# A fused attention and expert kernel: its front end as a list of timed steps, ordered inside the kernel

## The chip, the cores and the metric

The kernel runs on one core of a Trainium2 chip. The metric is device time in microseconds (us) for one execution; lower is better. A run's time is that of the whole program; the profiled execution also gives the span from its first to its last instruction.

## What is computed

Three layers follow each other. An attention with 32 memory slots turns q, k, v and phi (4 batches, 8 heads, 576 rows, 64 columns) into x, 2304 tokens of 512 numbers. A layer of eight experts then sends each token to its two best experts. A last layer multiplies, applies g = h cos h and multiplies again.

```python
a = softmax(phi, axis=rows)                     # 4 x 8 heads, 576 x 32
k_m, v_m = a^T k, a^T v                         # 32 x 64 for each head
x = softmax(q k_m^T / 8) v_m                    # 2304 tokens x 512
noisy = x @ w_gate + log1p(exp(x @ w_noise)) * noise
top2 = two largest of noisy                     # with weights from their softmax
out[token] = sum over its two experts of weight * (relu(x @ w1[e]) @ w2[e])
h = out @ w_in;  result = (h * cos(h)) @ w_out
```

## The kernel before, in words

**Keys.** For each of the four batches `k_gen` takes the maximum of phi on VectorE (DVE), the exponential on ScalarE (ACT), transposes the weights on TensorE (`et`), multiplies them with the batch's five row tiles of k and v in one matmul of 128 columns (`kp`), scales (`kd`, `vm`), transposes the keys (`pk`) and lays them block by block into `bdk`. The values go into `bdv`, four heads of a group side by side and masked, and 16 routing columns are appended. `sb` and `sT` hold a power of two by which x is scaled.

**Tiles.** For each of 18 tiles of 128 tokens `t_gen` does the scores (`sc`, TensorE), their maximum and subtraction (DVE: `smx`, `sd`), the exponential (ACT), the sum and its reciprocal (DVE: `ssm`), the product (`d`, GpSimd, called POOL here), a transpose (`pt`), its copy (`e2T`, ACT), the product with the values (`x`, two matmuls of 272 columns for a whole tile), the scaled copy (`xs`), the routing columns (`lgb` or `rt`), a 16-bit copy (`hl`, ACT), the rest of it (`hl` again, POOL), and a store to `xd` in memory. Tiles 4 and 13 hold rows of two batches.

**Routing.** `route(0)` handles tiles 0 to 7, `route(1)` tiles 8 to 17: a chain of some 40 small DVE steps that ends in tables made on TensorE (`rank`, then `tab` out of `ohp` and `oha`), and from them token lists `idxA` and `idxB`. POOL gathers the listed rows (`xg`) by an indirect transfer; a transposing transfer on the SP queue turns them into `x`.

**Experts.** Expert e works on part 0 (two blocks of 128 tokens, from tiles 0 to 7 alone) and part 1 (three blocks): `l1` (matmul `h`, eight groups of 12 matmuls for part 0) and `l2` (matmul `y`). Its weights are split into a 16-bit part `w` made on ACT after a sum of squares (`junk`, `sums`, `wsc`) and a rest made on DVE. Expert 0's part 0 runs before route(1) is done (`l2_first`), and from its part 1 on the TensorE has work without end.

**Order.** Every step has a time written out by hand (`a_of`, `t_steps`, `k_start`, `k_steps`); steps are recorded in the order of these times. Some instructions are also held behind a named earlier one (`gated`). Loads stand in a fixed list on SP's queue.

Of the kernel before, what the change touches and what calls it, by code (L numbers as in the profile page):

```python
# [60 lines left out]
def fused_kernel(ctx, tc, phiT, qT, kv, wgn, noise, w1, w2, wi, wo, out):  # L61
# [14 lines left out]
    line = []  # L76
    LEAD = dict(l1=60.0, l2=60.0, l1_out=60.0, l2_out=60.0, gather_x=50.0, turn_x=50.0)
# [36 lines left out]
    V.tensor_scalar(after, jp, 0.0, -1.0, op0=OP.is_le, op1=OP.mult)  # L114
    ones = sm([P, P], F16, "ones")
# [129 lines left out]
    def w_lo(i, c):  # L245
        scaled_lo(wt[i][:, 1, PIECE[c]], piece(i, c), wt[i][:, 0, PIECE[c]], i)
# [95 lines left out]
    def route(g):  # L342
# [4 lines left out]
        u, w1p, l, c, y = (rg(g, k, n, E) for k in "uwlcy")  # L347
        lgp = rg(g, "lgp", n, 2 * E)
        V.tensor_tensor(lgp, lgb[g][:, :, 0], lgb[g][:, :, 1], op=OP.add)
        gate, z = lgp[:, :, 0:E], lgp[:, :, E:]  # L350
        last["u"] = V.scalar_tensor_tensor(u, z, -1.0, z, op0=OP.mult, op1=OP.max)
        A.activation(u, u, AF.Exp, scale=-1.0)
        yield
        last["w1p"] = V.tensor_scalar(w1p, u, 1.0, None, op0=OP.add)
        last["ln"] = A.activation(l, w1p, AF.Ln)
        yield
        V.scalar_tensor_tensor(c, w1p, 1.0, u, op0=OP.subtract, op1=OP.subtract)
        V.reciprocal(w1p, w1p)
        V.tensor_tensor(c, c, w1p, op=OP.mult)
        V.scalar_tensor_tensor(c, z, 0.0, c, op0=OP.max, op1=OP.subtract)  # L360
        yield
        V.tensor_tensor(l, l, c, op=OP.add)
        V.tensor_tensor(l, l, noise_sb[:, ts, :], op=OP.mult)
        V.tensor_tensor(y, l, gate, op=OP.add)
        yield
        mk = [rg(g, f"m{k}", n) for k in range(2)]
        kx = rg(g, "k", n)
        for k in range(2):
            V.tensor_reduce(mk[k], y, axis=AX.X, op=OP.max)
            yield  # L370
            V.tensor_tensor(c, y, bc_t(mk[k], n), op=OP.is_equal)
            yield
            V.tensor_tensor(c, c, bc_e(ekey, n), op=OP.mult)
            yield
            V.tensor_reduce(kx, c, axis=AX.X, op=OP.max)
            yield
            V.tensor_tensor(oh[k][:, ts, :], c, bc_t(kx, n), op=OP.is_equal)
            yield
            if k == 0:
                V.scalar_tensor_tensor(y, oh[0][:, ts, :], -3.0e38, y, op0=OP.mult, op1=OP.add)  # L380
                yield
        last[f"m16{g}"] = V.tensor_tensor(m16[:, ts, :], oh[0][:, ts, :], oh[1][:, ts, :], op=OP.add)
        d = rg(g, "d", n)
        V.tensor_tensor(d, mk[1], mk[0], op=OP.subtract)
        A.activation(d, d, AF.Exp)
        yield
        r = mbank("rank")
        w = n * E
        mv = m16[:, ts, :].rearrange("p t e -> p e t")
        T.matmul(r[:, 0:w], lhsT=after, rhs=mv, start=True, stop=False, skip_group_check=True)  # L390
        T.matmul(r[:, 0:w], lhsT=ones, rhs=e32[:, :, :n], start=False, stop=True, skip_group_check=True)
# [881 lines left out]
```

## Time and profile before

| what | value |
|---|---|
| median of three runs | 926.5 us (925.14 to 928.25) |
| the profiled execution, its own time | 926.95 us |
| its span | 925.1 us |
| TensorE (PE) busy | 879.5 us, 95% of the span |
| DVE, ACT, POOL busy | 582.4, 467.7, 215.4 us |

The profiled execution's own time is 1.85 us more than its span. An engine's busy time counts its instructions, not its waits. The granted clock is TensorE's: 1.00 stands for 2.4 GHz and 0.50 for 1.2 GHz.

### The profile page before, as it was taken

The page shows a single profiled execution, that of the slowest core. Times are in us where ns is not written, and L with a number is a line of the kernel's source. Part 1 is how long each engine was busy: PE and PEld are TensorE (multiplying, and loading weights), DVE is VectorE, ACT ScalarE, POOL GpSimd, SP SyncE. Part 2 cuts the span into 40 slices and gives each one's busy share as a digit, 9 for nine tenths or more (in the row PEclk, how much of TensorE's full clock was granted, in tenths as well). Part 3 has the DMA queues.
Part 4 walks back from the last instruction along what each step waited for, and adds up shares of the span by engine and source line. Part 5 has one row for each costly group of instructions (what it writes and reads, how often), then busy time and mean ns, then how long its engine had stood idle before and what let it go on. Part 6 is the DMA issues. An engine that isn't in the chain of part 4 may idle for free. (4 is left out here: it accounts for less than half of the span.)

```text
span 925.1 us, 14179 instructions
## 1 busy us (share of the span) xinstructions
PE 879.5 (95%) x5368; PEld 511.0 (55%) x5368; DVE 582.4 (63%) x1266; ACT 467.7 (51%) x830; POOL 215.4 (23%) x234
## 2 busy tenths in 40 slices
PE   5997499999999999999999998999999999999997
PEld 4875355746566574756555565664444444444564
DVE  3668753766657575766571377787875765554564
ACT  3588426666666676777761334444333432422242
POOL 1355222110201101020000034434322521322221
PEclk9897599999999999999999999999999999999999
DMA  9982469787778979696762553322301610200010
GB/s 353 395 300 86 114 167 263 240 291 236 237 257 252 289 242 282 231 307 247 205 216 93 171 160 58 95 52 72 80 1 12 149 23 12 68 12 1 1 46 23
DMA packets 108246, 146.55 MB, mean 158 GB/s; under 512 B 65808, under 2 KB 66448, under 8 KB 106128
## 3 DMA queue, kind: packets, MB, share of 16 engines
q1 hardware_dynamic: 89536, 103.56, 36.5%
q0 software_dynamic: 6080, 19.93, 7.5%
q10 hardware_dynamic: 12560, 22.13, 6.7%
q8 instruction: 43, 0.70, 0.3%
q14 instruction: 27, 0.22, 0.1%
HBM read 95.26 MB, written 35.13 MB: 141 GB/s over the span
## 5 line engine op out<-in xcount | busy, mean ns | idle before, releaser
L219 PE MATMUL h<-x,w 128*128 128x384 f16 (+1 forms) x1536 | 215.3, 302 | 9.8 <-DMA x<-xg 9.2
L219 PE MATMUL y<-w,hT 128*128 128x512 f16 x960 | 210.7, 379 | 2.2 <-issue 2.2
L219 PE MATMUL g<-x2T,win 128*128 128x256 f16 (+1 forms) x1152 | 203.8, 327 | 5.5 <-DVE ty L1048 4.9
L219 PE MATMUL o<-wout,gT 128*128 128x512 f16 x864 | 202.5, 380 | 0.3 <-POOL gT L1050 0.2
L219 PEld LDWEIGHTS <-w 128*128 128x128 f16 x1536 | 151.5, 99 | 68.9 <-DMA x<-xg 8.8
L219 PEld LDWEIGHTS <-win 128*128 128x128 f16 x1152 | 113.2, 98 | 89.8 <-issue 6.8
L219 PEld LDWEIGHTS <-hT 128*128 128x128 f16 x960 | 93.9, 99 | 111.4 <-issue 2.7
L1050 POOL TENSOR_TENSOR gT<-ty,gT 128x256 f16<-128x256 f32 (+1 forms) x96 | 92.9, 968 | 253.8 <-ACT gT L1049 249.9
L1047 ACT ACTIVATE tt<-tt,hp 128x256 f32<-128x256 f32 (+1 forms) x96 | 58.9, 614 | 163.8 <-DVE tt L1046 147.7
L219 PEld LDWEIGHTS <-gT 128*128 128x128 f16 x864 | 84.4, 98 | 93.8 <-POOL gT L1050 1.9
L219 DVE SCALAR_TENSOR_TENSOR w<-raw,wsc,w 128x1024 f16<-128x1024 f32 x64 | 81.1, 1288 | 32.8 <-ACT w L219 31.2
L219 DVE SCALAR_TENSOR_TENSOR hT<-h,hT 128x384 f16<-128x384 f32 (+1 forms) x128 | 61.4, 487 | 61.9 <-ACT hT L219 61.7
L1044 DVE SCALAR_TENSOR_TENSOR ty<-g,wis,bct 128x256 f32<-128x256 f32 (+1 forms) x96 | 58.9, 613 | 65.1 <-PE g L219 65.1
L219 ACT ACTIVATE hT<-h 128x384 f16<-128x384 f32 (+1 forms) x128 | 55.2, 435 | 74.3 <-PE h L219 70.2
L1048 DVE SCALAR_TENSOR_TENSOR ty<-g,fac,tt 128x256 f32<-128x256 f32 (+1 forms) x96 | 59.1, 616 | 53.0 <-ACT tt L1047 52.5
L1049 ACT ACTIVATE gT<-ty 128x256 f16<-128x256 f32 (+1 forms) x96 | 50.2, 523 | 66.0 <-DVE ty L1048 65.9
L829 POOL DMA_INDIRECT xg<-xd,idxB x24 | 25.1, 1045 | 218.3 <-DMA x<-xg 206.9
L219 ACT ACTIVATE w<-raw,wsc 128x1024 f16<-128x1024 f32 x64 | 71.6, 1140 | 4.1 <-DVE wsc L219 1.9
L219 ACT ACTIVATE junk<-raw 128x1024 bf16<-128x1024 f32 x64 | 67.3, 1052 | 3.8 <-ACT o L219 2.5
L1046 DVE SCALAR_TENSOR_TENSOR tt<-tt,ty 128x256 f32<-128x256 f32 (+1 forms) x96 | 67.5, 703 | 2.6
L219 ACT ACTIVATE o<-y,ysc 128x512 f32<-128x512 f32 x40 | 27.5, 687 | 73.3 <-PE y L219 73.3
L968 POOL DMA_INDIRECT y<-yd,sidx x36 | 36.2, 1004 | 88.4 <-DMA yd<-o 80.7
(234 smaller groups left out, 712.8 us busy)
## 6 DMA issues: line engine op xcount, KB each, us to landing
raw<-in_w SPq DMA_DIRECT2D x32, 1024.0 KB, 11.4
yd<-o ACTq DMA_DIRECT2D x40, 256.0 KB, 6.8
kvt<-in_kv SPq DMA_DIRECT2D x9, 1024.0 KB
cvt<-in_wi SPq DMA_DIRECT2D x8, 1024.0 KB
wst<-cvt SPq DMA_DIRECT2D x16, 512.0 KB
cvt<-in_wo SPq DMA_DIRECT2D x8, 1024.0 KB, 8.6
yd<-zero ACTq DMA_DIRECT2D x13, 512.0 KB, 7.1
xd<-hl SPq DMA_DIRECT2D x18, 256.0 KB, 2.0
```

Of the source, the lines that this page charges most:

```text
L219: last[key] = fn(*a, **kw)
L829: G.indirect_dma_start(out=g, out_offset=None, in_=xd[0:NA * P] if part == 0 else xd, in_offset=bass.IndirectOffsetOnAxis(ap=idx[:, col:co ...
L968: G.indirect_dma_start(out=y, out_offset=None, in_=yd[0:rows], in_offset=bass.IndirectOffsetOnAxis(ap=sidx[:, t, k:k + 1], axis=0))
L1044: V.scalar_tensor_tensor(y, ph[:, :n], wis[:, 2 * E + c:2 * E + c + 1], bct[j], op0=OP.mult, op1=OP.mult)
L1046: V.scalar_tensor_tensor(t, t, MAGIC, y, op0=OP.subtract, op1=OP.subtract)
L1047: A.activation(t, t, AF.Sin, bias=hp, scale=-2.0 * math.pi)
L1048: V.scalar_tensor_tensor(y, ph[:, :n], fac[:, c:c + 1], t, op0=OP.mult, op1=OP.mult)
L1049: A.activation(g[:, 0, :n], y, AF.Copy)
L1050: G.tensor_tensor(g[:, 1, :n], y, g[:, 0, :n], op=OP.subtract)
```

## The change

The generators and the hand-written times of the front end go. Each step (one key step, one tile step, one route step, one load) becomes an entry of a list: engine, duration, function, the entries that it waits for. `settle` lays the entries out engine by engine, forwards and backwards in turn, and keeps the layout in which expert 0's part 1 starts earliest. Every instruction of a step is then chained to the one before it on its engine, so that this order stands in the program.

```diff
+    def op(eng, cost, fn, *deps, lat=None):
+        ...
+        plan.append((eng, cost, fn, [d for d in flat if d is not None], LAT[eng] if lat is None else lat))
+        return len(plan) - 1
+    def settle(goal):
...
+        best = now = place([-x for x in tail], before)
+        for _ in range(ROUNDS):
+            end = place([-(t + c) for t, c in zip(now, cost)], after)
+            last_end = max(t + c for t, c in zip(end, cost))
+            now = place([last_end - t - c for t, c in zip(end, cost)], before)
+            if now[goal] < best[goal]:
+                best = now
+        for i in sorted(range(n), key=lambda i: (best[i], i)):
+            if plan[i][2]:
+                at(best[i], plan[i][2])
```

Beside the order these things change.

```diff
 first batch: keys of three row blocks are loaded before their values; its kp becomes kp and vp, 64 columns each
+    def load_kv(j, half=None):
...
+        cs = slice(0, 2 * DM) if half is None else slice(half * DM, half * DM + DM)
+        load(kvt[j][:, :, cs], kv[2 * j * P:2 * (j + 1) * P, cs].rearrange("(t p) d -> p t d", p=P))
 values: halves of the contraction rows
-        bv = ap.tile([P, 2, 272], F32, tag="bdv", name="bdv")
+            x = bdv[b] = ap.tile([P, 2, 144], F32, tag="bdv", name="bdv")
-                    last[f"t{t}P"] = T.matmul(x[pn, g, 0:272], lhsT=eT[:, g, pn], rhs=bdv[b][:, g, :], start=True,
-                                              stop=True)
+                    for j in range(2):
+                        pj = slice(64 * j, 64 * j + 64)
+                        chain("P", T.matmul, c["x"][pn, j, 144 * g:144 * g + 144], lhsT=c["eT"][pj, g, pn],
+                              rhs=bdv[b][pj, g, :], start=True, stop=True)
 from other engines to POOL: the 16-bit copy of tiles 6 to 13, sT, the product with tokb
+            if t in HI_POOL:
+                chain("G", G.tensor_copy, c["hv"][:, 0], c["xs"])
+            else:
+                chain("A", A.activation, c["hv"][:, 0], c["xs"], AF.Copy)
-        V.tensor_copy(sT[:, :, full[0]:full[-1] + 1], sb[:, :, None].to_broadcast([P, 2, n]))
+            chain("G", G.tensor_copy, sT[:, :, full[0]:full[-1] + 1], s[:, :, None].to_broadcast([P, 2, n]))
-            V.tensor_tensor(oha, oha, tokb[:, tt, None, None].to_broadcast([P, m, 2, nc_]), op=OP.mult)
+                chain("G", G.tensor_tensor, x, x, tokb[:, t:t + m, None, None].to_broadcast([P, m, 2, nc_]), op=OP.mult)
 TensorE is given 21 matmuls of 512 columns before there is data
+    def keep_busy(n):
+        w = mbank("busy")
+        for k in range(n):
+            chain("P", T.matmul, w, lhsT=ones, rhs=ones[:, None, :].to_broadcast([P, 4, P]), start=True, stop=True,
+                  skip_group_check=True)
+    o_busy = op("P", 6.2, lambda: keep_busy(21))
 expert 0, part 1: the gathered rows are turned on TensorE, no longer by a transposing transfer
+    def turn_on_pe(e, part, c):
+        z = turned[c] = bank_y().bitcast(F16).rearrange("p (k t) -> p k t", k=8)
+        for k in range(8):
+            chain("P", T.transpose, z[:, k, :], xg[e, c][:, k * P:(k + 1) * P], ident16)
+    def turn_out(e, part, c, half):
...
+        if half:
+            chain("V", V.tensor_copy, xT[e, part][:, ks, cs], turned[c][:, ks, :])
+        else:
+            chain("A", A.activation, xT[e, part][:, ks, cs], turned[c][:, ks, :], AF.Copy)
 what follows is placed from the layout's own start of expert 0, part 1
-    X = [a_end + 0.5]
+    X = [x_first]
```

What the layout makes of three places is seen in the instruction rows; the number at the end of a row says how often it stands.

**TensorE, the first batch.** Before, all products of weights with keys and values come first, then the first keys are turned and the first scores follow:

```order
L577 MATMUL et<-ident,ew 128x128 x10
L589 MATMUL kp<-kvt,e 32x128 x40
L601 MATMUL pk<-ident,kd 128x128 x2
L616 MATMUL pv<-ident,vm 64x128 x2
L659 MATMUL sc<-bdk,qt 128x64 x4
```

Now, behind the 21 matmuls into `busy`:

```order
L291 MATMUL et<-ident,ew 128x128 x8
L291 MATMUL vp<-kvt,e 32x64 x8
L291 MATMUL kp<-kvt,e 32x64 x16
...
L291 MATMUL kp<-kvt,e 32x64 x8
L291 MATMUL vp<-kvt,e 32x64 x8
L291 MATMUL pk<-ident,kd 128x128 x2
L291 MATMUL sc<-bdk,qt 128x64 x4
```

Products with the keys (`kp`) and with the values (`vp`) alternate by row tile, a value product is the first, and the turn of the keys (`pk`) stands behind the last value product.

**POOL, around the first gathers.** Before, both gathers of expert 0's part 0 stand behind the work of all 18 tiles:

```order
L705 TENSOR_TENSOR hl<-xs,hl 128x512
L412 CAST af<-af_125 128x16
L705 TENSOR_TENSOR hl<-xs,hl 128x512 x4
L829 DMA xg<-xd,idxA 128x1024 x2
L412 CAST af<-af_125 128x20
```

Now (`sd_148` is tile 15's, `sd_145` tile 16's, `sd_146` tile 17's):

```order
L291 TENSOR_TENSOR d<-sd_148,ssm 128x256
L291 DMA xg<-xd,idxA 128x1024
L291 TENSOR_TENSOR d<-sd_145,ssm 128x256
L291 TENSOR_TENSOR d<-sd_146,ssm 128x256
L291 DMA xg<-xd,idxA 128x1024
L291 TENSOR_TENSOR hl<-xs,hl 128x512 x4
L291 CAST af<-af_127 128x20
```

The second gather stands right behind tile 17's product, ahead of the last four tiles' `hl`.

**TensorE, the last table of route(1).** Before, the products `tab` are spread among the groups of `h`, and the last two stand ahead of all of `y`:

```order
L219 MATMUL h<-x_1393,w 128x256
L433 LDWEIGHTS ohp
L433 MATMUL tab<-oha,ohp 128x24
L433 LDWEIGHTS ohp
L433 MATMUL tab<-oha,ohp 128x24
L219 LDWEIGHTS hT
L219 MATMUL y<-w,hT 128x512
```

Now 18 of the 20 stand behind all of `h`, and the last two behind 32 of the 48 matmuls of `y`:

```order
L291 MATMUL y<-w,hT 128x512
L291 LDWEIGHTS ohp
L291 MATMUL tab<-oha,ohp 128x24
L291 LDWEIGHTS ohp
L291 MATMUL tab<-oha,ohp 128x24
L291 LDWEIGHTS hT
L291 MATMUL y<-w,hT 128x512
```

`idxB` needs the last `tab`, so it has moved behind 32 matmuls of `y`. The `rank` matmuls of route(1), which stood behind two groups of `h`, now stand behind six.

## Rows read from the trace of the kernel before

**Rows 1.** Windows: us, busy PE, PEld, DVE, ACT, POOL, clock, DMA share, GB/s.

```profile
132.50:925.10 792.60, 778.15 (x4446) 435.86 (x4445) 498.91 (x970) 392.60 (x644) 167.91 (x167) 1.00 0.48 146
...
18.80:30.00 11.20, 11.07 (x129) 8.98 (x128) 4.86 (x19) 3.99 (x11) 1.24 (x2) 0.55 1.04 401
30.00:81.10 51.10, 46.62 (x497) 37.44 (x498) 36.53 (x116) 43.05 (x119) 27.46 (x34) 1.00 0.75 279
81.10:95.50 14.40, 9.39 (x38) 5.82 (x36) 10.45 (x48) 11.68 (x25) 6.38 (x7) 0.51 0.24 91
18.80:81.10 62.30, 57.69 (x625) 46.42 (x624) 41.39 (x134) 47.04 (x130) 28.70 (x36) 0.92 0.80 301
```

**Rows 2.** Timeline of PE, first batch: start, us, instruction, idle before and releaser.

```profile
13.28 2.79 PE L589 MATMUL kp<-kvt,e 128*32 128x128 f32 x48 [0.73 <-DMA kvt<-in_kv]
...
18.79 1.00 PE L659 MATMUL sc<-bdk,qt 128*128 128x64 f32 x8
```

**Rows 3.** Timeline of PE at the full clock, two places where matmuls follow directly.

```profile
41.82 0.64 PE L589 MATMUL kp<-kvt,e 128*32 128x128 f32 x14
42.39 1.10 PE L659 MATMUL sc<-bdk,qt 128*128 128x64 f32 x8
...
51.10 1.14 PE L689 MATMUL x<-bdv,e2T 128*128 128x272 f32 x4
52.08 0.38 PE L577 MATMUL et<-ident,ew 128*128 128x128 f32 x2
```

**Rows 4.** Timelines of DVE and POOL: route steps beside POOL's work, one of them twice.

```profile
69.93 1.11 DVE L354 TENSOR_SCALAR rw<-ru 128x64 f32<-128x64 f32 x1 [0.24 <-ACT ru L352]
...
81.59 0.61 POOL L675 TENSOR_TENSOR d<-sd,ssm 128x256 f32<-128x256 f32 x1 [1.42 <-DVE rc L373]
82.25 1.15 POOL L705 TENSOR_TENSOR hl<-xs,hl 128x512 f16<-128x512 f32 x1
82.32 1.16 DVE L382 TENSOR_TENSOR m<-oh,oh 128x64 f16<-128x64 f32 x1
...
106.32 0.24 DVE L382 TENSOR_TENSOR m<-oh,oh 128x80 f16<-128x80 f32 x1
```

**Rows 5.** Windows of DVE's lines 638, 642 (`sT`) and 427 (`tokb`).

```profile
18.80:81.10 62.30, 1.86 (x4) 0.92 0.80 301
...
18.80:81.10 62.30, 1.57 (x4) 0.92 0.80 301
...
81.10:95.50 14.40, 1.10 (x3) 0.51 0.24 91
```

**Rows 6.** Timelines of DVE, POOL, PE: tile 17's sum to expert 0.

```profile
80.68 0.42 DVE L672 TENSOR_REDUCE ssm<-sd 128x8 f32<-128x264 f32 x1
...
98.54 1.89 POOL L829 DMA_INDIRECT xg<-xd,idxA  x1 [0.30 <-issue]
...
106.43 5.30 PE L219 MATMUL h<-x,w 128*128 128x256 f16 x24 [8.71 <-DMA x<-xg]
```

**Rows 7.** Timelines of PE, DVE, POOL after that, and one landing time.

```profile
111.73 0.31 PE L392 MATMUL rank<-m,ones 128*128 128x80 f16 x1
111.86 4.15 PE L219 MATMUL h<-x,w 128*128 128x256 f16 x36
...
119.71 0.30 PE L433 MATMUL tab<-oha,ohp 128*128 128x24 f16 x6
...
121.52 10.52 PE L219 MATMUL y<-w,hT 128*128 128x512 f16 x48
132.54 2.76 PE L219 MATMUL h<-x,w 128*128 128x384 f16 x16 [0.49 <-DMA x<-xg]
...
121.71 0.18 DVE L441 TENSOR_TENSOR idxB<-tab,tabB 128x24 int32<-128x24 f32 x1 [0.83 <-PE tab L433]
...
124.82 0.94 POOL L829 DMA_INDIRECT xg<-xd,idxB  x1 [0.30 <-issue]
...
xg<-xd,idxB POOLq DMA_INDIRECT x3, 3.6
```

More of the change, by code (lines that the diff above doesn't have):

```diff
@@ L356, in route @@
[L356 to L367, printed above, removed]
@@ L392, in route, with tiles @@
-        last["rank"] = T.matmul(r[:, w:2 * w], lhsT=ones, rhs=mv, start=True, stop=True, skip_group_check=True)
-        yield
-        upto = rg(g, "cum", w)
-        V.tensor_tensor_scan(upto, same[g], r[:, w:2 * w], 0.0, op0=OP.mult, op1=OP.add)
+        w = n * E
+        early = n - 2
+        q = {}
+        def tiles():
+            for k in "uwlcy":
+                q[k] = rg(g, k, n, E)
+            q["lgp"] = rg(g, "lgp", n, 2 * E)
+            q["gate"], q["z"] = q["lgp"][:, :, 0:E], q["lgp"][:, :, E:]
+            q["mk"] = [rg(g, f"m{k}", n) for k in range(2)]
+            q["kx"], q["d"], q["cum"] = rg(g, "k", n), rg(g, "d", n), rg(g, "cum", w)
+            q["vk"], q["den"] = rg(g, "vk", n, 2), rg(g, "den", n)
@@ new lines, in lgp, with make @@
+        def lgp(a, b):
+            def make():
+                if not q:
+                    tiles()
+                return [red(q["lgp"][:, a:b], lgb[g][:, a:b].rearrange("p t s n -> p t n s"), OP.add)]
+            return make
+        o = v(0.9, lgp(0, early), o_rt[t0 + early - 1], *([o_free["rt"]] if g else []))
+        o = v(0.27, lgp(early, n), o, o_rt[t1 - 1])
+        o = v(0.27, lambda: [stt(q["u"], q["z"], -1.0, q["z"], op0=OP.mult, op1=OP.max)], o)
+        o = a_(0.25, lambda: chain("A", A.activation, q["u"], q["u"], AF.Exp, scale=-1.0), o)
@@ new lines, in places, with make, table, run @@
+        def places(t):
+            def make():
+                x = q["ohp", t] = small.tile([P, 2, P], F16, tag="ohp", name="ohp", bufs=4)
+                return [ts_(x[:, k], iota_r, pf[:, t, k:k + 1], None, op0=OP.is_equal) for k in range(2)]
+            return make
+        def table(t, q_):
+            def run():
+                if t == t0:
+                    q["tb"] = mbank("tab")
+                for k in range(2):
+                    chain("P", T.matmul, q["tb"][:, :nc_], lhsT=q["ohp", t][:, k], rhs=q["oha", t - q_][:, q_, k],
+                          start=(t == t0 and k == 0), stop=(t == t1 - 1 and k == 1))
+            return run
@@ new lines, in gather @@
+    def gather(e, part, c):
+        idx = idxA if part == 0 else idxB
+        if c == parts[part][0]:
+            n = parts[part][1] - parts[part][0]
+            xT[e, part] = xp.tile([P, 8, n * P], F16, tag=f"x{part}", name=f"x{part}")
+        xg[e, c] = xp.tile([P, 2 * DM], F16, tag="xg", name="xg", bufs=3)
+        col = e * (parts[part][1] - parts[part][0]) + c - parts[part][0]
+        chain("G", G.indirect_dma_start, out=xg[e, c], out_offset=None, in_=xd[0:NA * P] if part == 0 else xd,
+              in_offset=bass.IndirectOffsetOnAxis(ap=idx[:, col:col + 1], axis=0))
@@ new lines, in fused_kernel @@
+    get_phi(1)
+    keys(0)
+    get_kv(3)
+    get_kv(4)
+    get_q(4, 8)
+    get_phi(2)
+    keys(1)
+    o_free["kv5"], o_free["kv6"] = o_free["used0"], o_free["used1"]
+    for t in range(5):
+        tile_ops(t)
+    get_kv(5)
+    get_kv(6)
+    get_q(8, 12)
+    get_phi(3)
+    keys(2)
+    o_free["rt"] = o_free["used5"]
+    for t in range(5, 9):
+        tile_ops(t)
+    get_kv(7)
+    o_free["kv8"] = o_free["used2"]
+    get_kv(8)
+    get_q(12, 16)
+    get_q(16, 18)
+    get_w(0, 0)
@@ L831, in gather_x @@
             if turn:
[L832 to L834 removed]
+                SP.dma_start_transpose(out=xT[e, part][:, :, (c - c0) * P:(c - c0 + 1) * P], in_=g)
     def turn_x(e, part, c):
```

811 lines of the change are left out of this document (496 added, 315 removed).

## The prediction

> **What bounds the kernel now.** I read the windows first, then the timelines. From 132.50, where expert 0's part 1 starts, TensorE is busy for 778.15 of 792.60 us at the full clock [rows 1]. This stretch keeps its code, so it keeps its 792.6 us, and the question is how much earlier it can start. Ahead of it TensorE is the busiest engine from the first score (18.79 [rows 2]) to the sum of the last tile, tile 17 (80.68 [rows 6]): 57.69 of 62.30 us [rows 1]. But 11.07 of these lie between 18.80 and 30.00, where the granted clock is 0.55, nearly always the lower of its two levels (1.2 GHz), and from 81.10 to 95.50 it is 0.51 [rows 1]. From that sum to expert 0's first matmul at 106.43 TensorE mostly waits; a transfer releases it [rows 6]. A last stretch, 106.43 to 132.54, holds `h`, the last tables and `y`, and ends with three gathers [rows 6, 7]. The change works on all three stretches.
>
> I make the sum against the profiled execution: span 925.1, time 926.95, which lies 0.05% above the median of the three runs. Two times closer than 0.3% (2.8 us) I call the same.
>
> **First score: 16.0 (18.79 before).** Before, the third load of keys and values lands at 13.28, with the products waiting for it [rows 2]; 0.59 + 3 x 1.05 MB have then come. The turn of the keys (`pk`) stands behind the last value product, so loading keys first does not let it start before the last value half. Ahead of that half come the same bytes and one more part of q, 0.52 MB; at 401 GB/s [rows 1] that is 1.3 us, so 14.6. Eight half products, the scale, the turn and its copy: 1.4 us, estimated. Bounds: 14 (the products catch up at once) and 18.8 (no gain).
>
> **First score to tile 17's sum: 56 us (61.9 before).** I take each engine's work in this stretch.
>
> TensorE: 57.69. If its first 11.07 run at the full clock they take half, minus 5.5. The product `x` now has 4 x 144 columns in two halves of the rows, where it had 2 x 272. It took 0.98 (51.10 to 52.08 [rows 3]). No row shows halves of the rows. Halves that follow each other would need as much as before; halves that overlap fully, 0.49. The nearest row is `kp`, which works on quarters of the columns: seven matmuls of 128 columns in 0.57 [rows 3], 0.08 each, while one of 272 columns takes 0.49 (the trace counts two instructions for a matmul of this type). That is a third of the time for its columns, so overlap between parts is real here; I take 0.6, minus 0.38 for some 15 tiles, 5.7. Tables of route(0) that now fall into the stretch: plus 1. Sum 47.5, bounds 42 and 59 (lower clock, no overlap).
>
> DVE: 41.39, and as the whole of route(0) now ends ahead of that sum, the 10.45 of the window behind it too [rows 1]. Moved to POOL: `sT` 1.86 + 1.57, `tokb` 1.10 [rows 5]. That leaves 47.3.
>
> POOL: 28.70 [rows 1]. Added: eight 16-bit copies, which no row shows at this size. Bounds 0.61 (half the elements, two inputs) and 1.16 (the same elements, two inputs [rows 4]); one input and all elements lie between, 0.9, together 7.2. Plus `sT`, `tokb` and one more `hl`, 5.7; minus half of three batches' `bdv`, 1.8. Sum 40: of 56 us 70%, where it was 46%.
>
> That share costs DVE something. A route step that starts while POOL works can last as long as POOL's instruction: the step `m` takes 1.16 beside an `hl` of 1.15 that ends with it, and 0.24 where POOL is idle [rows 4]. From 69.93 to 82.32 there are five such steps [rows 4], which lose about 4 us in all. At 70 instead of 46 that is 6, plus 2: DVE 49.4.
>
> The Trainium skill (SBUF — State Buffer, "Who interferes with whom") gives this as a lock: DVE with two inputs from SBUF, or in a two-port mode, and GpSimd hold a port pair for a whole instruction, and the later one stands still. The `m` row agrees; that only five steps show it does not settle how often. Applied to every route step it speaks against moving work to POOL; its sum is a rival below.
>
> ACT: 47.04, minus eight copies of about 0.6, plus some of the work behind: 45. So DVE becomes the longest. An engine in a chain of four is not full: TensorE before was at 93% [rows 1]. With 88% for DVE, 49.4 / 0.88 = 56. Bounds 51 (93%, no added locks) and 65. Tile 17's sum comes at 16 + 56 = **72**.
>
> **That sum to expert 0's first matmul: 9 us (25.8 before).** The second gather stands on POOL behind tile 17's product: the sum, its reciprocal and 0.61 for the product [rows 4] make 1.2. From that gather's start to the first matmul it took 7.9 (98.54 to 106.43 [rows 6]). So 9.1, and the first `h` at **81**. Beside it lies the splitting of the expert's weights, which now also begins after tile 17's sum: about 0.5 for the scale, 2 for ACT's tile work, four splits, one rest, some 8.4 in all by my estimate. If the gather is quicker, this is late next.
>
> **First `h` to part 1: 34 us (26.1 before).** Here the order costs. `rank` of route(1) stands behind six groups of `h` where it stood behind two. TensorE has waited some 4 us when `h` starts, so I expect the lower clock for the first two groups, as before: 5.30 for 24 matmuls, then 4.15 for 36 [rows 6, 7], that is 5.3 + 5.5 = 10.8. `rank` 0.5. From `rank` (111.73) to the last `tab` but two (120.0) it took 8.3 [rows 7]; `tokb` leaves DVE, so 7.7. Then 32 of 48 matmuls `y`, 7.0 of 10.52 [rows 7], stand ahead of the last `tab`; before, none did. Table and `idxB` 0.4. From `idxB` to the third gather 3.1 (121.71 to 124.82), landing 3.6 [rows 7]: 6.5 counted from its end. Turning on TensorE replaces the transposing transfers: eight transposes and a copy, for which I take 1.3. No row has 16-bit transposes of 128 columns; bounds 0.6 and 2.5. Before, from the landing (128.4) to 132.54 it was 4.1, so this edit gives back 2.8. Sum 10.8 + 0.5 + 7.7 + 7.0 + 0.4 + 6.5 + 1.3 = 34.2.
>
> The 7 us of `y` are not lost to TensorE as work, since `y` had to be done; what is lost is the cover: before, `y` ran while the gathers were under way, now only its last 16 matmuls do. Behind `idxB` on DVE nothing waits; the four rests of expert 0's second weights stand ahead of it (5.2) but end before the 32 matmuls do.
>
> **Sum.** Part 1 starts at 81.1 + 34.2 = 115.3 instead of 132.54: minus 17.2. 926.95 - 17.2 = **910**.
>
> **Rivals.**
>
> *Everything fits.* The 21 early matmuls bring the full clock, no locks are added, DVE runs at 93%: sum of tile 17 at 16 + 51 = 67, first `h` at 76, and at the full clock (six groups in 8.3) 31.7 to part 1. 107.8, minus 24.7: **902**. For it: TensorE, which was the busiest, loses a fifth of its work. Against: all four engines would then be busy above 75% of the stretch.
>
> *The locks, by the page's rule.* If every one of route(0)'s 41 DVE steps that meets POOL (70%) waits for half an instruction of 0.9, that is 13 us where I count 6; the sum comes at 79, `h` at 88, and with `y` too at the lower clock (2.5 more) part 1 starts at 125: **919**. A first batch at the lower clock, as now until 30, would add 5.5 on TensorE, which stays below DVE then.
>
> *Slower.* One mechanism: DVE stands still for whole POOL instructions. `m` lost 0.92. If all 41 steps do, that is 38 us, and part 1 starts at 147: 941. It decides from a loss of 0.64 a step on, where tile 17's sum comes at 92 and part 1 at 135.3. Against it: the five steps counted above lost 4 us together, and they stand among some 25 route steps of the same stretch, so the mean loss before is below 0.2 a step.
>
> *The order does not hold.* A chained order is as good as its durations; a step that is late holds all behind it on its engine. If that takes 17 us in sum, nothing changes: **927**.
>
> **How the numbers follow.** Forecast (905 to 917) 0.49; everything fits (899 to 905) 0.20; locks (917 to 922) 0.16; no change 0.05; slower 0.07; the rest, 0.03, lies below 899. The likeliest is 910. From 900 to 922 about 0.8 lie: the first three without their ends. Faster by more than 0.3% 0.88, same 0.05, slower 0.07.
>
> **What the profile will show.** First score near 16, with the clock at 1.00 between 18 and 30 (TensorE) if the early matmuls work. `x` of a tile in about 0.6. Tile 17's sum near 72, DVE the busiest engine ahead of it, and more route steps of 0.8 and longer beside POOL. The second gather right behind the last `d`. First `h` near 81, part 1 near 115, with TensorE idle between the last `h` and the first `y`. From there 792.6 to the end. The prediction is wrong if the tile stretch is not bound by DVE, or if the rest does not keep its length because expert 1's weights, loaded at another time, come late.

## The result, and the profile after

The changed kernel took **936.25 us** (median of 4 runs, 935.59 to 939.22), the kernel before, run beside it, 926.81 (925.14 to 928.25): a ratio of 1.011, 95% interval 1.008 to 1.014. It is 1.1% slower, where 910 was forecast. The profiled execution is the longest of the four, 939.22 with a span of 937.4.

The forecast was a chain of five stages, so I read them first. The windows of the changed kernel (the stretch and its length, busy time of each engine, granted clock, busy share of the DMA engines, GB/s):

```profile
143.70:937.40 793.70, 781.36 (x4446) 436.69 (x4445) 498.30 (x971) 392.14 (x643) 164.82 (x166) 0.99 0.47 141
21.80:30.00 8.20, 8.20 (x93) 7.33 (x94) 3.20 (x10) 3.62 (x10) 1.23 (x2) 0.60 1.04 397
30.00:60.00 30.00, 26.21 (x358) 21.25 (x356) 21.16 (x61) 24.12 (x69) 15.22 (x24) 1.00 1.03 393
60.00:93.30 33.30, 25.53 (x269) 20.50 (x267) 28.44 (x93) 17.64 (x48) 21.29 (x33) 0.74 0.19 73
```

The engines are in the order TensorE, its weight loads, VectorE (DVE), ScalarE (ACT), GpSimd (POOL). Expert 0's part 1 starts at 143.7 and the rest lasts 793.7, nearly as before (792.6 [rows 1]). The early matmuls did not free the first tiles of the lower clock (0.60 until 30). The tiles have two parts: until 60 TensorE is busy for 34.41 of 38.20 us (8.20 + 26.21) and DVE for 24.36, and the loads keep the DMA engines full (1.03 to 1.04); from 60 to the last sum DVE is the busiest, for 28.44 of 33.30, and TensorE's granted clock is 0.74. Of the 18 sums the eleventh starts at 60.28 (56.22 before), and the seven behind it take 32.7 us (24.5 before).

Ahead of the first score, DVE's timeline shows what came late:

```profile
18.43 1.35 DVE L291 TENSOR_REDUCE mx<-ph 128x2 f32<-128x1152 f32 x1 [2.85 <-DMA ph<-in_phiT]
19.82 0.17 DVE L291 TENSOR_SCALAR mx<-mx 128x2 f32<-128x2 f32 x1
19.89 0.60 DVE L291 TENSOR_SCALAR kd<-kp,den 128x128 f32<-128x128 f32 x2
20.99 0.28 DVE L291 COPY bdk<-pk 64x128 f32<-64x128 f32 x1 [0.49 <-PE pk L291]
```

The maximum of the *second* batch's phi stands ahead of the scaling of the first batch's keys (`kd`) and waits until 18.43 for its load. The list had it at 11.7 (the start that its own planner gives it). The first batch's last key product had ended at 17.6.

TensorE's timeline from the first `h` to part 1:

```profile
102.05 10.39 PE L291 MATMUL h<-x,w 128*128 128x256 f16 x72 [1.95 <-DMA x<-xg]
113.72 0.30 PE L291 MATMUL rank<-m,after 128*128 128x80 f16 x1 [1.28 <-DVE m L291]
...
120.93 1.18 PE L291 MATMUL tab<-oha,ohp 128*128 128x24 f16 x7 [0.21 <-DVE ohp L291]
121.96 9.73 PE L291 MATMUL y<-w,hT 128*128 128x512 f16 x32
131.53 0.20 PE L291 MATMUL tab<-oha,ohp 128*128 128x24 f16 x2
131.59 3.61 PE L291 MATMUL y<-w,hT 128*128 128x512 f16 x16
135.58 0.62 PE L291 MATMUL y<-ident,xg 128*128 128x128 f16 x8 [0.38 <-DMA xg<-xd,idxB]
137.91 0.62 PE L291 MATMUL y<-ident,xg 128*128 128x128 f16 x8 [1.71 <-DMA xg<-xd,idxB]
142.01 1.03 PE L291 MATMUL y<-ident,xg 128*128 128x128 f16 x8 [3.49 <-DMA xg<-xd,idxB]
143.73 0.48 PE L291 MATMUL h<-x,w 128*128 128x384 f16 x1 [0.69 <-ACT x L291]
```

and POOL's, with the gathers of the second half, and those of the next expert behind them:

```profile
132.22 1.00 POOL L291 DMA_INDIRECT xg<-xd,idxB  x1 [8.61 <-DVE idxB L291]
133.53 0.95 POOL L291 DMA_INDIRECT xg<-xd,idxB  x1 [0.30 <-DMA raw<-in_w]
134.78 0.95 POOL L291 DMA_INDIRECT xg<-xd,idxB  x1 [0.30 <-issue]
136.47 0.94 POOL L1180 DMA_INDIRECT xg<-xd,idxA  x1 [0.75 <-PE y L291]
138.80 0.94 POOL L1180 DMA_INDIRECT xg<-xd,idxA  x1 [1.38 <-PE y L291]
```

The 32 matmuls `y` hold the last table for 9.73 us; TensorE then waits 3.49 for the third gather, issued at 134.78 and not there before 142.01 (3.6 us before [rows 7]).

### The profile page after: what moved, and what is told of

It is laid out like the page before. It is cut to its first block, busy times and chain, and to the rows that moved or that the text cites. A ratio compares the mean times of both kernels' runs of the same rounds, so it can differ in the third digit from the quotient of the medians.

```text
span 937.4 us, 14541 instructions
## 1 busy us (share of the span) xinstructions
PE 891.4 (95%) x5565; PEld 516.9 (55%) x5565; DVE 587.5 (63%) x1258; ACT 467.4 (50%) x825; POOL 219.9 (23%) x257
## 5 line engine op out<-in xcount | busy, mean ns | idle before, releaser
L291 PE MATMUL y<-w,hT 128*128 128x512 f16 x960 | 213.4, 382 | 2.1 <-issue 2.1
L291 PEld LDWEIGHTS <-w 128*128 128x128 f16 x1536 | 152.1, 100 | 63.3 <-issue 3.5
L291 DVE SCALAR_TENSOR_TENSOR w<-raw,wsc,w 128x1024 f16<-128x1024 f32 x64 | 80.7, 1281 | 34.7 <-ACT w L291 34.6
L1180 POOL DMA_INDIRECT xg<-xd,idxB x21 | 22.1, 1052 | 206.1 <-DMA x<-xg 199.8
L291 ACT ACTIVATE o<-y,ysc 128x512 f32<-128x512 f32 x40 | 27.5, 687 | 72.9 <-PE y L291 72.8
L1321 POOL DMA_INDIRECT y<-yd,sidx x36 | 35.7, 991 | 88.5 <-DMA yd<-o 80.8
```

Of the source, the lines that this page charges most:

```text
L291: last[key] = fn(*a, **kw)
L1180: G.indirect_dma_start(out=g, out_offset=None, in_=xd[0:NA * P] if part == 0 else xd, in_offset=bass.IndirectOffsetOnAxis(ap=idx[:, col:co ...
L1321: G.indirect_dma_start(out=y, out_offset=None, in_=yd[0:rows], in_offset=bass.IndirectOffsetOnAxis(ap=sidx[:, t, k:k + 1], axis=0))
```

## The experiments

All start from the changed kernel. One table first: time (ratio to the kernel before and its interval), then the stages of each profiled execution, worked out from five starts in its timelines: TensorE's first `sc`, DVE's last `ssm`, TensorE's first `h`, its first `h` of 384 columns, and the end of the span.

| kernel | median us | ratio | first score | to last sum | to first h | to part 1 | rest |
|---|---|---|---|---|---|---|---|
| before | 926.8 | | 18.8 | 61.9 | 25.8 | 26.1 | 792.6 |
| forecast | 910 | | 16.0 | 56 | 9.1 | 34.2 | 792.6 |
| changed | 936.3 | 1.011 [1.008, 1.014] | 21.8 | 71.1 | 9.1 | 41.7 | 793.7 |
| e1 casts on ACT | 936.2 | 1.011 [1.007, 1.014] | 21.4 | 70.4 | 9.4 | 40.3 | 792.2 |
| e2 POOL as before | 944.2 | 1.018 [1.014, 1.022] | 21.4 | 76.6 | 9.8 | 40.2 | 793.6 |
| e4 (same order) | 937.0 | 1.011 [1.008, 1.014] | 21.4 | 69.6 | 9.1 | 40.7 | 791.6 |
| e4b loads held | 938.0 | 1.014 [1.011, 1.017] | 21.6 | 69.6 | 9.2 | 41.4 | 791.6 |
| e5 tables later | 939.5 | 1.014 [1.010, 1.018] | 22.6 | 68.2 | 10.4 | 41.4 | 795.7 |
| e5b tables last | 941.7 | 1.017 [1.015, 1.019] | 23.9 | 63.3 | 17.4 | 42.0 | 794.4 |
| e3b y behind table | 934.5 | 1.007 [1.005, 1.010] | 21.4 | 71.5 | 9.5 | 35.7 | 793.0 |
| e8 busy early | 944.3 | 1.020 [1.018, 1.022] | 24.0 | 72.3 | 9.6 | 38.3 | 796.2 |
| e9 busy tiles | 940.5 | 1.015 [1.012, 1.019] | 22.8 | 70.9 | 10.1 | 40.3 | 793.0 |
| e10 DVE more early | 940.4 | 1.016 [1.015, 1.018] | 21.6 | 70.6 | 9.0 | 40.8 | 795.1 |
| e11 DVE more late | 942.0 | 1.017 [1.015, 1.019] | 21.5 | 71.4 | 9.0 | 43.0 | 795.3 |
| e12 DVE less late | 935.5 | 1.011 [1.009, 1.013] | 22.7 | 65.8 | 8.4 | 41.2 | 795.7 |
| e7b phi's maximum | 936.9 | 1.011 [1.009, 1.014] | 15.4 | 74.9 | 9.1 | 40.9 | 795.3 |
| e14 durations | 931.4 | 1.006 [1.004, 1.008] | 15.5 | 72.0 | 11.6 | 35.7 | 795.0 |
| e15 turned last | 941.0 | 1.015 [1.012, 1.018] | 21.3 | 69.0 | 12.1 | 40.7 | 795.6 |
| e13 combined | 926.9 | 1.002 [0.999, 1.004] | 17.4 | 64.6 | 11.9 | 38.4 | 791.8 |
| e16 all four | 928.0 | 1.002 [1.001, 1.004] | 17.1 | 72.9 | 14.9 | 31.0 | 792.6 |
| e17 order only | 927.7 | 1.002 [1.001, 1.003] | 15.4 | 71.8 | 13.2 | 32.7 | 792.9 |

`e4` kept the changed kernel's order (see below) and so shows how far one order's executions differ: 1.5 us in a stage, 2.1 in the rest. In `e3b`, `e5`, `e5b`, `e7b`, `e8` and `e13` to `e17` the list lays the front end out anew, so such a run differs from the changed kernel in more than its edit.

**Is it POOL's work?** `e1` makes the casts of tiles 6 to 13 on ACT, `e2` also gives `sT` and the `tokb` product back to DVE.

```diff
-            if t in HI_POOL:
-                chain("G", G.tensor_copy, c["hv"][:, 0], c["xs"])
-            else:
                 chain("A", A.activation, c["hv"][:, 0], c["xs"], AF.Copy)
...
-            chain("G", G.tensor_copy, sT[...], s[...])        # e2, and "G" to "V" for oha * tokb
+            chain("V", V.tensor_copy, sT[...], s[...])
```

> The sixteen-bit copies of tiles 6 to 13 are made on ScalarE in place of GpSimd, at the same places of the order; nothing else moves. Order theory (first scores to tile 17's sum grew from 61.9 to 71.1 us because the first batch's routing steps stand ahead of tiles 15 to 17): the stretch stays at 70 to 72 and the time within 1.5 us of the changed kernel's 936. Lock theory (GpSimd's eight added casts of 0.61 make VectorE's two-operand steps stand still): each cast taken away gives back up to its 0.61, so up to 4.9 us, the stretch at 66 to 68 and the time at 931 to 933. If ScalarE is the bound of these tiles the stretch gets longer, by up to 8 x 0.6 = 4.8.

> As the run before it, and the copy of the weights' sums (sT) and the routing weights' product back on VectorE, so that GpSimd does no more than in the kernel before. Order theory: stretch 69 to 72, time 934 to 938 (VectorE gets 18 copies of under 0.2 us and a few products back). Lock theory: all that GpSimd's added work costs comes back, the stretch at 64 to 67 and the time at 929 to 932.

The casts cost nothing that shows (936.2; 70.4 us). `e2` fits neither theory: with less on POOL (29.97 us busy in the stretch, 37.74 in the changed kernel) it is 8 us slower. The timelines of DVE and POOL in `e2` show one place where it loses:

```profile
44.29 0.37 DVE L291 TENSOR_REDUCE smx<-sc 128x8 f32<-128x256 f32 x1
44.58 0.61 DVE L291 COPY sT<-sb 128x8 f32<-128x8 f32 x1
45.20 1.09 DVE L291 COPY sT<-sb 64x2 f32<-64x2 f32 x1
46.32 0.42 DVE L291 TENSOR_TENSOR sd<-sc,smx 128x256 f32<-128x256 f32 x1
44.54 0.61 POOL L291 TENSOR_TENSOR d<-sd,ssm 128x256 f32<-128x256 f32 x1
45.12 1.15 POOL L291 TENSOR_TENSOR hl<-xs,hl 128x512 f16<-128x512 f32 x1
```

and TensorE's:

```profile
46.80 1.97 PE L291 MATMUL sc<-bdk,qt 128*128 128x64 f32 x8 [2.06 <-DVE sd L291]
48.70 1.08 PE L291 MATMUL kp<-kvt,e 128*32 128x128 f32 x16
```

Two copies stand between a tile's maximum and its subtraction for 1.71 us, and each of them ends with the POOL instruction beside it: 0.61 beside a `d` of 0.61, 1.09 beside an `hl` of 1.15. The other six copies of `sT` in `e2` take 0.15 to 0.17 each, so about 1.4 of the 1.71 us are DVE standing still beside POOL. A later score, which needs the buffer, waits 2.06, and behind this wait the rows are those of the lower clock: `sc` lasts 1.97 where it lasts 1.00 at the full one, `kp` 1.08 for 0.64. On POOL in the changed kernel the copies take 0.18 to 0.19 each and the casts 0.61 (my estimate was 0.9), as two groups of its tile stretch show (count, busy us, mean ns, idle time before them):

```profile
L291 POOL CAST hl<-xs 128x512 f16<-128x512 f32 x8 | 4.9, 609 | 7.1 <-ACT xs L291 7.1
L291 POOL COPY sT<-sb 128x8 f32<-128x8 f32 x4 | 0.8, 190 | 2.8 <-DVE sb L291 2.8
```

So neither run took this standing still away: the `d` and `hl` that DVE waits beside were on POOL before as well. It can be counted in the traces. In the changed kernel a step looks like this:

```profile
64.40 1.14 DVE L291 TENSOR_TENSOR rc<-ry,rm 128x64 f32<-128x64 f32 x1
64.31 1.15 POOL L291 TENSOR_TENSOR hl<-xs,hl 128x512 f16<-128x512 f32 x1
```

I count each DVE step of the tile stretch that ends with a POOL instruction and lasts over 0.1 us longer than the shortest of the same step in any run here, and add up what it lasts longer: 5.1 us (10 steps) before, 10.1 (21) in the changed kernel and 10.2 in `e4`, 8.3 in `e1`, 9.3 in `e2`, 5.1 in `e3b` (below), 6.7 in `e17` (below). It has doubled, but the length of the stretch does not follow it: `e3b` and `e17` have half and two thirds of it and take 71.5 and 71.8 us.

**Is it TensorE's clock?** `e9` puts six small matmuls of ones ahead of each product `x` from tile 9 on; `e8` fills the holes ahead of the first score.

```diff
             c["x"] = aps.tile([P, 2, 512], F32, tag="x", name="x")
+            for r in range(6 if t > 8 else 0):
+                chain("P", T.matmul, c["x"][:, r % 2, 288:512], lhsT=ones, rhs=<ones, 224 columns>, start=True, stop=True)
...
+                k["f1"] = op("P", 3.0, lambda: fill(10), k["et4"])        # e8: ahead of kp
+            k["f2"] = op("P", 0.8, lambda: fill(4), last_v)               # last value product; f3: the same behind pk
```

> Ahead of the product x of tiles 9 to 17 six small matmuls of ones (224 columns each) fill TensorE's waits for the copy that x needs. Clock theory (TensorE's lower clock from 68 us on is what stretches the last tiles): the granted clock of 68 to 93 is over 0.9 instead of 0.5 to 0.7 and the last tile's sum comes 3 to 5 us earlier, at 88 to 90; the time falls by 2 to 5. Rival (VectorE, which is busy for 9.3 of the 10 us from 60 to 70, sets these tiles): the clock may rise, but the sum stays within 1.5 us of 92.9, or later by the matmuls' own 5 us where TensorE is late; time 935 to 941.

> More matmuls of ones fill the three holes that TensorE has ahead of the first score (ten behind the transposes of the weights, four behind the last value product, four behind the turn of the keys), and the maximum of the second batch's phi waits on VectorE behind the scaling of the first batch's keys. Clock theory: the granted clock stays at 1.00 from 12 to 30 instead of 0.50 to 0.60; the first score comes at 19.5 to 20.5 instead of 21.8 and the fourth tile's score (33.5) 3 to 5 us earlier; the time falls by 2 to 4. Rival (the clock falls at 22 whatever was done before, or the loads, at 400 GB/s, set these tiles): clock 0.5 between 20 and 30 again, fourth tile's score within 1.5 us of 33.5, the time at 935 to 937.

The window of `e9` from 60 to the last sum, to be read beside the one of 60 to 93.3 above:

```profile
60.00:93.70 33.70, 27.26 (x307) 21.21 (x303) 28.48 (x93) 17.34 (x49) 21.31 (x33) 0.88 0.20 76
```

The clock rises from 0.74 to 0.88 and the stretch keeps its length (70.9): so a higher clock alone does not shorten the late tiles, though the added matmuls take time on TensorE as well and may eat part of a gain. `e8` also puts the maximum of phi behind the scaled keys. In it the clock was 0.50 from 20 to 24 all the same, behind a wait of 4.23 us for the exponential of phi, and the first score, at 24.0, came later; the time, 944.3, is above both expected ranges. The list was laid out anew around the added steps, so this run does not price the early clock.

**Is it DVE?** `e5` and `e5b` move the first batch's tables behind the sum of tile 17, and of both last tiles.

```diff
+    # after all tile_ops; wide and places also wait for tk[17]["su"] (e5), tk[17]["su"] and tk[16]["su"] (e5b)
     o_idxA, o_rank0 = route(0, kb[0]["vm"])
```

> The first batch's tables (places, wide rows, table products) wait for tile 17's sum, as the order of the kernel before had them. Order theory: the 7.1 us of places and wide rows that VectorE does between 65 and 93 us leave the tile stretch, tile 17's sum comes 7 to 9 us earlier (84 to 86), and the first h at 100 to 103, since the tables then follow: 9 us of stretch are traded for 9 of tables, and the time stays within 3 us of 936. Rival (the stretch is long because of locks or TensorE's clock, not because of these steps): the sum stays at 90 to 93 and the first h comes later by the tables, at 108 to 111, time 940 to 945.

> All of the first batch's tables (places, wide rows, table products) wait for the sums of both last tiles. Theory of two bounds: VectorE has the same work between 60 us and the first h wherever it stands, so the last tile's sum comes 7 to 9 us earlier (62 to 64 after the first score), the index of the first gather that much later behind it, and the first h within 2 us of 80.3 after the first score; the time stays within 3 of 936. Rival (putting the tables ahead of the last tiles is what made the kernel slow): the first h comes 4 us earlier or more and the time is under 932.

In `e5` tile 16's sum was planned behind the tables, so the last sum came only 1.4 to 2.9 us earlier; in `e5b` it comes 6 to 8 earlier, and the tables follow. From the first score to the first `h` it is 78.6 and 80.7 us, 80.3 in the changed kernel: the place of the tables moves time between two stages. The times, 939.5 and 941.7, are 0.5 and 2.7 us above what was expected. The prices then, on DVE alone: seven sums done twice early (`e10`) or late (`e11`), and tiles 11 to 17 without maximum and subtraction (`e12`, which leaves these out).

```diff
             chain("V", V.reciprocal, c["su"], c["su"])
+            if t in range(2, 9):                  # e11: range(11, 18)
+                chain("V", V.tensor_reduce, <scratch>, c["dk"], axis=AX.X, op=OP.add)
...
+            if t >= 11:                           # e12, in place of maximum, subtraction and exponential
+                chain("A", A.activation, c["dv"], c["sv"], AF.Exp, scale=0.125)
```

> VectorE does the sum of each of tiles 2 to 8 twice (seven reductions of 0.42 us more, 2.9 in all, the second into a scratch tile). Theory of two bounds (ahead of 60 us TensorE and the loads set the tiles, VectorE being 64% busy; behind it VectorE does, 87% busy): these 2.9 us are hidden, the last tile's sum stays within 1 us of 71.1 after the first score, the time within 2 of 936. Rival (the whole stretch is one chain of waits between the engines, any addition is paid): 2 to 3 us later, time 938.5 to 940.

> The same for tiles 11 to 17 (2.9 us more on VectorE). Theory of two bounds: the last tile's sum comes 2.5 to 3 us later after the first score (73.6 to 74.1) and the time rises by about as much, to 938.5 to 940. Rival (the late stretch is set by TensorE's lower clock or by latency): under 1 us later and the time within 2 of 936.

> Tiles 11 to 17 leave out the row maximum and its subtraction ahead of the exponential (ScalarE reads the scores itself): 14 VectorE instructions of 0.41 to 0.42 us fewer, 5.9 us, at the same places of the order. Theory of two bounds: the last tile's sum comes 4.5 to 6 us earlier after the first score (65 to 66.6 instead of 71.1), and the time is 930 to 932. Rival (lower clock): no more than 2 us earlier, 934 to 936.

The windows of `e11` and of `e12` from 60 to the last sum:

```profile
60.00:92.90 32.90, 24.94 (x231) 19.65 (x232) 28.62 (x96) 16.37 (x45) 20.15 (x31) 0.72 0.18 69
```

```profile
60.00:88.50 28.50, 25.33 (x243) 20.71 (x235) 23.27 (x77) 16.25 (x45) 20.38 (x32) 0.69 0.21 79
```

Added early, 2.9 us are hidden in the stretch (70.6). Taken out late, 5.9 give 3.8 to 5.3 there, at a clock no better (0.69). Added late, 2.9 cost 0.3 to 1.8, less than the theory wanted: 4 to 5 us in which DVE waits take part of it up. So DVE's work counts late, above all where it lies in a tile's own chain. That is read from the stage; the times do not bear it out. By its ratio `e12` is level with the changed kernel (1.011 both) and `e10` 0.5% behind it, close to what their rivals had, and `e11`, at 942.0, is above both expected ranges. The rests of `e10` and `e12`, 795.1 and 795.7, are at the long end of 791.6 to 796.2; nothing here says what sets that.

**What holds part 1?** `e3b` puts all `y` behind the last table and the turning behind `y`; `e4` and `e4b` keep three raw weight loads from the gathers' neighbourhood; `e15` turns the first gathered piece last.

```diff
-    y1 = [op("P", 3.5, lambda c=c: l2_first(c, False), h_done, hi1, o_pools, s1) for c in range(CA)]
+    y1 = [op("P", 3.5, lambda c=c: l2_first(c, False), h_done, hi1, o_pools, s1, o_last_tab) for c in range(CA)]
-        o = op("P", 0.55, lambda c=c: turn_on_pe(0, 1, c), o, y2 if c == NST - 1 else [], o_pools)
+        o = op("P", 0.55, lambda c=c: turn_on_pe(0, 1, c), o, y2, y3[:c - CA], o_pools)    # y3: l2_out
...
                 z = SP.dma_start_transpose(out=xT[e, part][...], in_=g)
+                if part == 0:
+                    last["load"] = z               # e4b: the loads are chained behind this transpose
```

> All 48 matmuls y of expert 0's first rows stand behind the second batch's last table, and the turning of the gathered rows on TensorE behind all of y, as in the kernel before. Order theory: the index of the second gather comes 8 to 9.7 us earlier after the first h (20 to 21 instead of 29.7), y (10.5 us at the full clock, up to 14 at half) then covers the gathers, and part 1 starts 35 to 38 after the first h instead of 41.7; the time falls by 4 to 7, to 929 to 932. Rival (the y that stood ahead of the table only filled a wait for VectorE, which sets the last tables): the index comes less than 3 us earlier and the time stays within 2 of 936.

> The first raw weight load of the fourth expert is issued only when the last transpose of the second gather's rows is done, so that it and the loads queued behind it on the sync engine's queue are out of the way of the second gather. Contention theory: the third gather of the second half lands 3.6 us after its issue as in the kernel before, not 7.2 after, part 1 starts about 3.5 us earlier (140), and the time falls by 3 to 3.5 to 933, unless the loads are then late for their expert. Rival, gather slow by itself or the products late because TensorE's clock is low: landing stays at 7 us and part 1 at 143 to 144; the time is 936, or later if the loads come late.

> The three raw weight loads (experts 1 and 2) stand on the sync engine's queue behind the two transposing transfers of the next expert, so none is under way beside the second gather's second half. Contention theory: the third gather lands 3.6 to 4.5 us after its issue instead of 7.2, part 1 starts 2.7 to 3.6 earlier after the first h (38 to 39 instead of 41.7), the time is 932.5 to 934. Rival (the gather is slow beside the other gathers, or by itself): the landing stays at 7 and the time at 936.

> Of the three gathered pieces of the second half the first is turned last, so that the next expert's gathers, which wait for its buffer, start only when all three have landed. Theory (the third gather is slow because the next expert's gathers run beside it): it lands 3.6 to 5 us after its issue instead of 7.2 to 7.8, and part 1 starts 2 to 3.5 us earlier behind the last index (9 to 10 us, instead of 11.9 to 12.5); time 933 to 934. Rival (it is slow by itself): no change.

The hold of `e4` had no effect: every queue kept its order, and the run is a repeat. In `e4b` the loads do stand behind the transposes, and the third gather still lands 7.8 us after its issue: it is slow without the weight loads too. `e15` did not reach its aim: the next expert's first gather is issued at 136.38, 1.7 us behind the third (134.64), as in the changed kernel, so it shows nothing. `e3b` on TensorE:

```profile
121.82 0.21 PE L291 MATMUL tab<-oha,ohp 128*128 128x24 f16 x2 [0.65 <-DVE rt L291]
121.88 13.40 PE L291 MATMUL y<-w,hT 128*128 128x512 f16 x48
135.11 1.55 PE L291 MATMUL y<-ident,xg 128*128 128x128 f16 x24
138.04 1.14 PE L291 MATMUL h<-x,w 128*128 128x384 f16 x6 [1.38 <-ACT x L291]
```

The last table comes 19.4 us after the first `h`, not 29.5; `y` covers the gathers, the three pieces are turned without a wait, and part 1 starts 5 to 6 us sooner after the first `h`. Of these the median keeps 1.8 (9 runs, 928.5 to 936.0; by the ratios it is 3), less than the 4 to 7 expected.

**Is it the list's durations?** `e7b` puts phi's maximum behind the first batch's keys; `e14` also lays the list out with durations nearer to the measured ones; `e13` is `e7b` and `e3b` with no tile's maximum subtracted, `e16` adds the durations to it, `e17` is `e16` with maximum and subtraction in place.

```diff
-        k["mx"] = op("V", 1.5, mx, landed[f"phi{b}"], g_("ex1"))
+        k["mx"] = op("V", 1.5, mx, landed[f"phi{b}"], g_("ex1"), g_("bkV") if b == 1 else None)
...
-    RATE = 400.0
+    RATE = 375.0                                    # e14, e16, e17: KB per us of a load
-            return op("V", cost, run, *deps)
+            return op("V", 1.4 * cost, run, *deps)  # the routing steps
-        k["hi"] = op("G", 0.9, hi, k["xs"], g3("stD")) if t in HI_POOL ...
+        k["hi"] = op("G", 0.61, hi, k["xs"], g3("stD")) if t in HI_POOL ...
```

> The maximum of the second batch's phi stands on VectorE behind the first batch's scaled keys and their turned copy, instead of ahead of them; the list is laid out anew. Theory (planned for 11.7 us, that step waits for a load that lands at 18.4 and holds the keys behind it): keys scaled at about 17.8 instead of 19.9, first score at 19.3 to 19.9 instead of 21.4 to 22.8, the time 1 to 2 us lower if the tiles keep their rate. Rival (the first tiles are set by the loads, or by TensorE at half its clock, whatever the first score): first score earlier, but the fourth tile's score stays at 31.6 to 33.5 and the time at 935 to 938.

> The edit of phi's maximum, and the list laid out with durations nearer to the measured ones: loads at 375 KB per us instead of 400, routing steps on VectorE 1.4 times as long, GpSimd's casts 0.61 instead of 0.9. Theory (the order is bad because its durations are): the last sum comes 3 us earlier or more than in the kernel with that edit alone, part 1 at 137 to 139, the time 930 to 933. Rival (the order is about as good as any; the work and the waits of the engines set the time): within 2 us of that kernel.

> Three edits together: the maximum of phi as in the run before this one; y behind the last table, turning behind y; and no tile has its row maximum subtracted (ScalarE takes the exponential of the scores themselves, which are small enough here). By the sum of the parts: first score 19.5 (21.5 to 22.8), last sum 65 later (70 to 71), sum to first h 8.5 to 9, first h to part 1 36: part 1 at 129 to 131 and the time 924 to 928, no worse than the kernel before (926.5). If VectorE's work is not what sets the late tiles, part 1 at 134 or later and the time 930 or more.

> The combined run's three edits with the measured durations of the run after it. If the gains add up: the measured durations gave 5.4 us (931.4 against 936.9), so part 1 at 127 to 128 and the time 921 to 923, below the kernel before (926.6). If both reach the same limit (the late tiles' chain with VectorE's work, of which the one takes away the subtraction and the other the badly placed steps), no gain over the combined run: 925 to 928.

> The same without leaving out the row maxima: the edit of phi's maximum, y behind the last table, and the measured durations, so that the changed kernel's computation is complete and only its order differs. If order and durations are the whole loss: part 1 at 130 to 132, 925 to 927, level with the kernel before. If VectorE's work late in the tiles is a limit of its own: part 1 at 132.5 to 135, the time 928 to 931.

TensorE's timeline of `e7b`, two rows of scores:

```profile
15.35 2.00 PE L291 MATMUL sc<-bdk,qt 128*128 128x64 f32 x16
...
28.34 1.08 PE L291 MATMUL sc<-bdk,qt 128*128 128x64 f32 x8
```

and DVE's, behind the keys:

```profile
13.35 0.28 DVE L291 COPY bdk<-pk 64x128 f32<-64x128 f32 x1 [1.44 <-PE pk L291]
19.23 1.35 DVE L291 TENSOR_REDUCE mx<-ph 128x2 f32<-128x1152 f32 x1 [5.60 <-DMA ph<-in_phiT]
20.62 0.17 DVE L291 TENSOR_SCALAR mx<-mx 128x2 f32<-128x2 f32 x1
20.70 0.42 DVE L291 TENSOR_REDUCE smx<-sc 128x8 f32<-128x256 f32 x1
```

The first score is 6 us earlier and buys nothing: the third stays at 28.3 (28.5 in `e4`, 30.3 in the changed kernel), and the time at 936.9. The step that held the keys has moved one place on and now holds the first tile: the maximum of the second batch's phi waits 5.60 us for its load, and the maximum of the first tile's scores stands behind it. On TensorE the third score, of a tile of the first batch, stands behind the second batch's transposes and products, which wait for the same load. A layout with the first tiles ahead of that step was not tried. `e14` is 5.4 us faster than `e7b` by three numbers of the list and nothing else; which of them did it I did not try. `e13` came out at 926.9, in the range expected of the sum of its parts (924 to 928), but with part 1 at 132.3, later than the 129 to 131 that the parts gave. `e16` gained nothing over it, and `e17`, which computes all that the changed kernel does, reaches 927.7, 0.2% above the kernel before and between the two ranges expected. TensorE's timeline of `e17`:

```profile
100.34 5.08 PE L291 MATMUL h<-x,w 128*128 128x256 f16 x24 [5.63 <-DMA x<-xg]
...
118.00 12.21 PE L291 MATMUL y<-w,hT 128*128 128x512 f16 x48
130.04 1.81 PE L291 MATMUL y<-ident,xg 128*128 128x128 f16 x24
133.03 2.27 PE L291 MATMUL h<-x,w 128*128 128x384 f16 x13 [1.18 <-ACT x L291]
```

Its part 1 starts at 133.03, half a microsecond behind the kernel before's 132.54. No version here beats the kernel before.

## Why the prediction was wrong

The profiled execution is 29.5 us longer than the sum of the forecast stages: 5.8 ahead of the first score, 15.1 in the tiles, 0 to the first `h`, 7.5 to part 1, 1.1 in the rest. In `e4`, the same order in a shorter execution, it is 24.5: 5.4, 13.6, 0, 6.5, -1.0.

**First score, 16.0: wrong, and worth nothing.** I took the loads of keys and values and TensorE's products. The step that failed is that nothing else stands ahead of the keys' turn: on DVE the second batch's maximum did, on a load that lands at 18.4. With it moved behind the keys (`e7b`) the score comes at 15.4, close to the forecast, but the step then holds the first tile's maximum on DVE, and the last sum comes at 90.3, where it came at 91.0 in `e4`.

**First score to last sum, 56: the step that failed is "49.4 / 0.88 = 56".** It takes each engine's work over the whole stretch and divides the longest by one share. DVE's term was 3.4 us too small: 52.80 us by the windows of 21.8 to 60 (24.36) and 60 to 93.3 (28.44). Its share is the larger error: 52.8 / 0.88 would still be 60, and DVE was busy for 74% of the 71.1 us. TensorE is nearly full in the first part (34.41 of 38.20), and DVE, which has nearly all of route(0) late, in the second; two parts with different limits add, 38 and 33, where I took the larger mean. In the first part the loads are full too, and no run tells which of the two sets it. TensorE's term was off too, 59.9 for 47.5 and beyond its bound of 59: the lower clock moved and grew (0.60 until 30, 0.74 behind 60) instead of going, and `x` takes 0.76 rather than 0.6. In the length of the stage `e10` and `e12` bear out the two parts, `e11` only in part; that they make the loss is argued from the windows, not shown by a run that takes one limit away. DVE's standing still beside POOL, which I priced at 6 us and as a rival at 13, counts 10.1: it explains DVE's larger term. It does not explain the length of the stretch, which stays at 71.5 with 5.1 us of it in the layout of `e3b`; how much of it lies on the path was not measured. The Trainium skill (SBUF — State Buffer, "Who interferes with whom") lets a DVE instruction stand still for a GpSimd one. The rows of single steps agree: `rc` lasts 1.14 us at 64.40 beside an `hl` of 1.15, and 1.16 at 68.70 beside another, where a step of the same shape takes 0.22 without one.

**Sum to first h, 9.1: right**, 9.1, against 25.8. The gather started 1.6 behind the sum (1.2) and the first `h` 7.5 behind that (7.9), so two small misses cancel.

**First h to part 1, 34.2: the mechanism right, two terms mis-sized.** `h` took 10.4 (10.8), the wait for `rank` 1.3 (0.5), from there to the first `y` 8.2 (7.7). The two that were mis-sized: the 32 `y` took 9.7 instead of 7.0, part of them at the lower clock (0.66 from 120 to 130), and the third gather 7.2 instead of 3.6. `e3b` shows the order's price: 5 to 6 us in the stage.

**Rest, 792.6: right** for the changed kernel (793.7, and 791.6 in its repeat).

**The rivals.** The slower one had the sign right and not the cause: it needs 0.64 us lost in each of 41 steps, 26 us, and the count gives 10. "The order does not hold" came nearest: a step with too early a time holds all behind it. I let it stop at no change. In the profiled execution the other stages lose the 16.7 us gained at the gather and 12 more. Three edits to the order alone (`e17`) take 8.5 of the 9.4 us of loss away, or 7.6 when each is set against the kernel before that ran beside it.

**Still open.** `e17`'s tiles take 71.8 us, 10 more than before, though its time is back; I did not find which of the moved steps keeps them there. Beside the third gather run two stores of `y` (issued at 134.28 and 135.95) and the next expert's gathers; which of them slows it was not separated. In `e3b` these come only from 134.35 on, two weight loads are issued beside it (125.15 and 127.59), and it lands after 6.2 us: more than one neighbour can slow it.

## What to carry to other kernels

Where a stretch has several limits in turn, cut it at the point where the busiest engine changes and add the parts; one mean share over the whole of it promises time that no part has. In a program whose queues are chained in a planned order, check each step's planned time against the landing of its load and against the duration that a trace shows: one step planned early, or one that stands still beside another engine between a maximum and its subtraction, holds its queue, and TensorE waits and runs at its lower clock behind it. Follow an early gain to the next thing that waits: the first score's 6 us ended at the same step, one place on in DVE's queue, and the gather's 16.7 were lost in the stages on either side.

## What the runs showed of the hardware

Two copies of a few numbers took 0.61 and 1.09 us on DVE where each ended with a POOL instruction (`sT` in `e2`), and 0.15 to 0.17 elsewhere on DVE; on POOL they took 0.18 to 0.19. Behind a wait of 2.06 us TensorE's rows show the lower clock, and added matmuls raised the granted clock of the late tiles (0.74 to 0.88) without giving time. Three gathers with others and stores close behind them landed after 3.3, 4.3 and 7.2 us; with the weight loads out of the way the third took 7.8.
